# Scores and values in groups of four units: a fused top-k attention and leaky-ReLU MLP kernel on one core

## The chip, the cores and the metric

The kernel runs on one core of a Trainium2 chip. A core has five engines that run side by side, each with its own queue of instructions: PE (TensorE, matmuls; the loading of its stationary operand is listed as PEld), DVE (VectorE), ACT (ScalarE), POOL (GpSimd) and SP (SyncE, which issues the transfers here). They wait for each other by semaphores. The metric is the device time of one execution in microseconds (us); lower is better. The median of three runs before the change is 1473.3 us (1473.19 to 1473.83).

## What is computed

Top-k attention over 8 batches of 8 heads, 576 queries and keys of 64 elements, and then an MLP on its output, all in float32:

```python
scores = q @ k.T / sqrt(64)                      # (8, 8, 576, 576)
kth = the 32nd largest score of each row
scores = where(scores >= kth, scores, -1e9)
attn = softmax(scores)                           # with + 1e-9 in the denominator
x = (attn @ v), heads side by side               # (4608 tokens, 512)
h = x @ w_in                                     # (4608, 2048)
out = maximum(0.01 * h, h) @ w_out               # (4608, 512)
```

## The kernel before

The attention is cut into 144 *units*: 128 query rows of a pair of heads each (or, where 576 is no multiple of 128, 64 rows of two pairs: the *left* units, two at the end of each even batch and two at the start of each odd one). The tokens of the MLP are cut into *chunks*: two of 128 tokens, then seventeen of 256; eight units fill a chunk of 256. The host code only lays the inputs out.

What is done for a unit, cut to its instructions:

```python
def scores(us):                       # two units at a time
    narrow = ps_sc.tile([P, 2, 512], F32, name="narrow")            # PSUM
    for k, u in enumerate(us):
        wide = ps_sc.tile([P, 2, 512], F32, name="wide", bufs=2)    # PSUM, two buffers
    ...  # PE: q by k; u0 wide part, u0 narrow part, u1 narrow part, u1 wide part
    ...  # ACT: copies the four parts to u.both ("s_sb"), in the same order (L227)

def top_k(u):                         # DVE; yields after each of 4 rounds ("slots")
    pairs = max and min of the row's two halves                     # L250
    for r in range(4):
        nc.vector.max(u.tops[..r..], ...)                           # L255, both heads
        if r < 3: nc.vector.match_replace(...)                      # L258, both heads
        yield

def mask(u, i):                       # POOL, head i of the unit: needs the last top
    pen = (u.s[i] < kth) * MASKED; u.s[i] += pen                    # L268, L269

def exponents(u, i):                  # ACT
    u.s[i] = exp(SCALE * u.s[i] + nbias), row sum to u.z            # L272
def sums(u):        u.ze = u.z + 1e-9                               # ACT, L277
def reciprocals(u): u.rz = 1 / u.ze                                 # DVE, L281
def normalize(u, i): u.s[i] *= u.rz                                 # ACT, L284

def transpose(u):                     # by way of DRAM
    for h in range(2):                # the two 16-bit halves of each word
        nc.scalar.copy(split, pairs[:, :, h])                       # ACT, L293
        nc.sync.dma_start(apart[:, h, :], split)
    u.wT = work.tile([P, 2 * NKC - 1, P], F32, name="wT", bufs=3)
    nc.sync.dma_start_transpose(out=u.wT.bitcast(U16), in_=apart...)
# transpose_in_haste / keep_transposed: the same on PE and ACT, for units 15, 23, 31

def weigh_values(u, po): ...          # PE: v by wT into PSUM (L333); po is in a "wide" buffer
def keep_values(u, po): ...           # ACT: po to x, the MLP's input (L347)
```

The MLP is a generator that yields after every few matmuls, so that the main loop can spread it between the attention's parts:

```python
def hidden_of_few(x):                 # the two chunks of 128 tokens
    for j in range(NFC // 4 + 1):
        if j < NFC // 4:
            ...                       # PE: quarter j of x @ w_in into ph
            nc.scalar.activation(g_of[j], ph, AF.Prelu, alpha=SLOPE)
            yield 2 * 512
        if j:
            ...                       # PE: quarter j-1 turned into pt; ACT: copied to gT
            yield 2 * P

def mlp(ch):
    ...                               # chunks of 256: ph (L384), Prelu to gT (L390), 8 times
    for r0 in range(0, n, P):
        for f in range(NFC):
            ...                       # PE: pz += gT[f] by w_out[f] (L396)
        ...                           # ACT: o_sb <- pz (L403); transfer to out
```

And the main loop, one unit per step; the instructions of each engine run in this order:

```python
def values_at(n):
    if n < UNHURRIED:
        return (n | 1) + LAG + 1, MIDDLE
    return (n | 1) + LAG - ((n | 1) in HURRIED), END       # LAG = 3

for s in range(len(steps) + LAG + 1):
    cur, old, older, new = unit(s), unit(s - 1), unit(s - 2), ()
    if s % 2 == 0:
        new = [u for u in steps[s + 2:s + 4] if u]
    slot()                            # DVE: first round of top_k(cur)
    mask(old, 0); mask(old, 1)        # POOL
    weights_of(older)                 # DVE: reciprocals; ACT: normalize x2 (from step 20 on)
    mlp_steps(budget)
    ...                               # values(s, MIDDLE) of the early steps
    slot()
    mlp_steps(budget)
    exponents(old, 0)
    transpose(older)
    slot()
    mlp_steps(budget); mlp_steps(budget)
    slot()
    mlp_steps(budget)
    exponents(old, 1); sums(old)
    keep(values(s, END), s, END)      # PE: two units' values; ACT: copies to x
    if new: scores(new)               # PE and ACT
    mlp_steps(budget); mlp_steps(budget)
    load_more(s)
```

`budget` is the MLP work at hand by the slots (seven per step) that are left until the next chunk is complete.

Before all this the weights arrive as 64-bit words, through three raw buffers, and are rounded to float32.

Of the kernel before, what the change touches and what calls it, by code (L numbers as in the profile page):

```python
# [16 lines left out]
NKC = 5  # L17
# [3 lines left out]
def kernel(  # L21
# [39 lines left out]
    loads = ctx.enter_context(tc.tile_pool(name="loads", bufs=LOADED))  # L61
    raws = ctx.enter_context(tc.tile_pool(name="raws", bufs=3))
    work = ctx.enter_context(tc.tile_pool(name="work", bufs=2))
# [18 lines left out]
    gT = const.tile([P, NFC, CHMAX], F32, name="gT")  # L82

# [4 lines left out]
    def piece(n):  # L90
# [5 lines left out]
        return w_out[f // 4][:, f % 4:f % 4 + 2, :].rearrange("p g n -> p (g n)")  # L96

    raw_of = {}

    def load_weights(n):  # L100
        if n >= NPIECE:
            return
        if not AS_WORDS:
            nc.sync.dma_start(piece(n), weights[n])
            return
        raw_of[n] = raws.tile([P, WCH, 4], U16, name="raw")
        nc.sync.dma_start(raw_of[n].rearrange("p n w -> p (n w)"), weights[n])

    def round_weights(n):
# [8 lines left out]
        low = raw.rearrange("p n w -> p (n w)").bitcast(U32).rearrange("p (n w) -> p n w", w=2)[:, :, 0]  # L118
        top = raws.tile([P, WCH], U16, name="top", bufs=2)
        scale = raws.tile([P, WCH], U16, name="scale", bufs=2)  # L120
        parts = work.tile([P, 2 * NKC - 1, P], F32, name="wT", bufs=3)
        parts = parts.rearrange("p c n -> p (c n)").bitcast(U16)
        m_top, m_low = parts[:, 0:WCH], parts[:, WCH:2 * WCH].bitcast(BF16)
        nc.gpsimd.tensor_copy(top, raw[:, :, 3])
        nc.scalar.activation(dst, mid, AF.Copy, bias=-7.0 - 2.0 ** -16, scale=2.0 ** -20)

        nc.scalar.activation(m_low, low, AF.Copy, bias=128.0, scale=2.0 ** -29)
        yield
        nc.vector.tensor_scalar(scale, top, 4, 0x7FF, ALU.logical_shift_right, ALU.bitwise_and)
# [31 lines left out]
    def load_qk(pi):  # L161
        if pi % (LOADED + 3) < LOADED:
            qt = loads.tile([P, S], F32, name="qt")
            kt = loads.tile([P, S], F32, name="kt")
        else:
            raw = raws.tile([P, WCH, 4], U16, name="raw").rearrange("p n w -> p (n w)").bitcast(F32)
            qt, kt = raw[:, 0:S], raw[:, S:2 * S]
        nc.sync.dma_start(qt, qT[pi])
        nc.sync.dma_start(kt, kT[pi])
        qk_of[pi] = qt, kt  # L170
# [32 lines left out]
    def scores(us):  # L203


        narrow = ps_sc.tile([P, 2, 512], F32, name="narrow")
        ps = {}
        for k, u in enumerate(us):
            wide = ps_sc.tile([P, 2, 512], F32, name="wide", bufs=2)
            ps[u] = ((wide[:, :, 0:WIDE], 0, WIDE),  # L210
                     (narrow[:, :, k * NARROW:(k + 1) * NARROW], WIDE, S))

        order = ((us[0], 0), (us[0], 1), (us[1], 1), (us[1], 0))
        for u, part in order:
            to, k0, k1 = ps[u][part]
            for n in range(0, len(u.parts), 2):
                for i, pi, side, r0 in u.parts[n:n + 2]:
                    qt, kt = qk_of[pi]
                    d = slice(side * D, (side + 1) * D)
                    nc.tensor.matmul(to[r0:r0 + u.rows, i, :], qt[d, u.q0:u.q0 + u.rows],  # L220
                                     kt[d, k0:k1], start=True, stop=True)
        for u in us:
            u.both = work.tile([P, 2, S], F32, name="s_sb", bufs=5)
            u.s = [u.both[:, i, :] for i in range(2)]
        for u, part in order:
            to, k0, k1 = ps[u][part]
            nc.scalar.copy(u.both[:, :, k0:k1], to)  # L227

    def first_scores(u):

        ps = [ps_sc.tile([P, 2, 512], F32, name="wide", bufs=2) for i in range(2)]
        for half in range(2):
            for i, pi, side, r0 in u.parts:
# [3 lines left out]
                                 kt[d, half * HS:(half + 1) * HS], start=True, stop=True)  # L237
        u.both = work.tile([P, 2, S], F32, name="s_sb", bufs=5)
        u.s = [u.both[:, i, :] for i in range(2)]
        for i in range(2):  # L240
# [45 lines left out]
    def transpose(u):  # L286
# [4 lines left out]
        for h in range(2):  # L291
            split = work.tile([P, 2 * S], U16, name="split", bufs=2)
            nc.scalar.copy(split, pairs[:, :, h])  # L293
            nc.sync.dma_start(apart[:, h, :], split)
        u.wT = work.tile([P, 2 * NKC - 1, P], F32, name="wT", bufs=3)
        nc.sync.dma_start_transpose(out=u.wT.bitcast(U16), in_=apart.rearrange("p h n -> (p h) n"))
# [12 lines left out]
    def keep_transposed(u):  # L309
        u.wT = work.tile([P, 2 * NKC - 1, P], F32, name="wT", bufs=3)  # L310
        for c0, c1, pt in u.parts_T:
            nc.scalar.copy(u.wT[:, c0:c1, :], pt[:, 0:c1 - c0, :])
# [37 lines left out]

    def hidden_of_few(x):

        g_of = {}
        for j in range(NFC // 4 + 1):
            if j < NFC // 4:
                ph = ps_ml.tile([P, 512], F32, name="ph", tag="ml")
                for c in range(HP):
                    nc.tensor.matmul(ph, x[c][:, 0:P], w_in[c][:, j * 512:(j + 1) * 512],
                                     start=(c == 0), stop=(c == HP - 1))
                    if c == 1:  # L360
                        yield 2 * 512
                g_of[j] = raws.tile([P, 2 * DMODEL], U16, name="scale", bufs=2).bitcast(F32)
                nc.scalar.activation(g_of[j], ph, AF.Prelu, alpha=SLOPE)
                yield 2 * 512
            if j:
                pt = ps_ml.tile([P, 4, P], F32, name="pt", tag="ml")
                for i in range(4):
                    nc.tensor.transpose(pt[:, i, :], g_of[j - 1][:, i * P:(i + 1) * P], ident)
                nc.scalar.copy(gT[:, 4 * (j - 1):4 * j, 0:P], pt)
                yield 2 * P  # L370

    def mlp(ch):
# [4 lines left out]
        if ch < EARLY:  # L377
            yield from hidden_of_few(x)
        for f0 in range(0, NFC if ch >= EARLY else 0, 2):
# [12 lines left out]
        for r0 in range(0, n, P):  # L392
            m = min(P, n - r0)
            pz = ps_ml.tile([P, 512], F32, name="pz", tag="ml")
            for f in range(NFC):
# [4 lines left out]
                if f % 2 and f + 1 < NFC:  # L400
                    yield 2 * DMODEL
            o_sb = work.tile([P, DMODEL], F32, name="o_sb", bufs=1)
            nc.scalar.copy(o_sb[0:m], pz[0:m, 0:DMODEL])  # L403
# [30 lines left out]
    HURRY = 20  # L434
    HURRIED = (15, 23, 31)
    UNHURRIED = 14
    MIDDLE, END = 0, 1

    def values_at(n):

        if n < UNHURRIED:
            return (n | 1) + LAG + 1, MIDDLE
        return (n | 1) + LAG - ((n | 1) in HURRIED), END

# [18 lines left out]

    def slot_budget(s):

        after = [at for (at, _), _ in ready_at if at >= s]
        until = after[0] if after else s
        if len(after) >= len(CHUNKS) - EARLY:
            return EARLY_SHARE
        return backlog[0] / ((until + 1 - s) * SLOTS)  # L470

    EARLY_SHARE = 500
    SLOTS = 7

    with tc.manual_schedule():
        last = {p: n for n, u in enumerate(steps) for p in u.pairs}

        def load_more(s):

            for of, load, n, lag in ((v_of, load_v, LOADED_V, LAG + 1), (qk_of, load_qk, LOADED + 3, 8)):  # L480
                while len(of) < NPAIR and (len(of) < n or last[len(of) - n] + lag <= s):
                    load(len(of))
                    if lag > LAG + 1 and len(of) > n:
                        break

# [4 lines left out]
        for n in range(NPIECE + 2):  # L490
            for i in (n, n - 1, n - 2) if AS_WORDS else ():
                if 0 <= i < NPIECE:
                    if i == n:
                        rounding[i] = round_weights(i)
                    next(rounding[i], None)
# [16 lines left out]
        def values(*place):  # L512
            due = [u for n, u in enumerate(steps) if values_at(n) == place]
            if due:
                po = ps_sc.tile([P, 2, 512], F32, name="wide", bufs=2)[:, 0, 0:2 * P]
                po = po.rearrange("p (u n) -> p u n", u=2)
            else:
                return ()
# [9 lines left out]
        for s in range(len(steps) + LAG + 1):  # L528
            cur, old, older, new = unit(s), unit(s - 1), unit(s - 2), ()
            if s % 2 == 0:  # L530
                new = [u for u in steps[s + 2:s + 4] if u]
            picks = top_k(cur) if cur else iter(())
            budget = slot_budget(s)

            def slot():
                next(picks, None)

            slot()
            if old:
                mask(old, 0)  # L540
                mask(old, 1)
            late = s < HURRY and not {s - 1, s - 2} & set(HURRIED)
            if older and not late:
                weights_of(older)
# [6 lines left out]
            if older and late:  # L551
                weights_of(older)
            if s - 2 in HURRIED:
                transpose_in_haste(older)
            mlp_steps(budget)
            if old:
                exponents(old, 0)
            if older:
                keep_transposed(older) if s - 2 in HURRIED else transpose(older)
            slot()  # L560
# [77 lines left out]
```

## Time and profile before

| | |
|---|---|
| median time | 1473.3 us |
| span of the profiled run | 1471.7 us |
| busy: PE, DVE, ACT, POOL | 1395.9, 1322.2, 1096.5, 1096.0 us |
| mean granted PE clock | 0.979 |
| PE busy in the first 240 us | 170.2 us |
| PE busy from 240 to 1400 us | 1157.9 of 1160 us |
| first to last top-k instruction on DVE | 64.7 to about 1385 us |

The busy share is a mean over stages. The table parts it: in the first 240 us the weights are loaded and rounded, and the first chunks wait for their units; after that PE has hardly a gap. The profile's queries used below are: the timeline (instructions of one engine in order of time, start and length in us, equal ones merged, with the idle time before them and what ended it), the waits (who waited for whom: us in total, times, longest) and the windows (busy time of each engine in a stretch, with the granted PE clock).

### The profile page before, as it was taken

The numbers are of one execution on the slowest core, as the hardware profiler recorded it, in microseconds if no ns is written. First come the engines' busy times: TensorE is split into PE (matmuls) and PEld (weight loads), VectorE is DVE, ScalarE is ACT, GpSimd is POOL, SyncE is SP. The second block draws the span as 40 slices with busy tenths as digits, with TensorE's granted clock in tenths as the row PEclk, the third lists the DMA queues.
The fourth block names the chain that finished last, engine by engine and source line by source line (L and its number), as shares of the span: only waits on it lengthen the run. The fifth ranks groups of instructions, "written<-read, shape, count | busy, mean of one in ns | idle before, by whom it ended". The sixth has DMA issues, their size and how long they took to land.

```text
span 1471.7 us, 24082 instructions
## 1 busy us (share of the span) xinstructions
PE 1395.9 (95%) x8059; PEld 928.4 (63%) x8059; DVE 1322.2 (90%) x3400; ACT 1096.5 (75%) x1979; POOL 1096.0 (74%) x743
## 2 busy tenths in 40 slices
PE   7717989999999999999999999999999999999998
PEld 2304547676767666666666666666666767676674
DVE  6999998999999999999999999999999999999600
ACT  8557877877787777777777777777777787877710
POOL 3288887888788888787878787888887888787600
PEclk9957999999999999999999999999999999999999
DMA  9725453654367554665466545565467655654510
GB/s 350 280 78 132 138 143 89 172 169 139 103 172 209 138 141 130 184 183 144 134 174 187 155 128 147 163 194 143 128 168 205 145 136 131 167 137 131 144 47 14
DMA packets 391419, 223.47 MB, mean 152 GB/s; under 512 B 336256, under 2 KB 336256, under 8 KB 389248
## 3 DMA queue, kind: packets, MB, share of 16 engines
q1 hardware_dynamic: 391296, 221.95, 54.0%
q8 instruction: 63, 1.03, 0.3%
q14 instruction: 60, 0.49, 0.1%
HBM read 46.14 MB, written 92.60 MB: 94 GB/s over the span
## 4 chain that ended last, share of the span: by engine, by line
PE 84%; DVE 10%; DMA 3%; ACT 2%; issue 1%; SPq 0%; POOL 0%; DVEq 0%; ACTq 0%
PE ph L384 32%; PE pz L396 32%; PE wide L333 11%; PE wide L220 6%; DVE tops L255 4%; PE narrow L220 3%; DVE pairs L258 3%; DMA wT<-apart 1%; DVE pairs L250 1%; DMA raw<-in_weights_dram 1%; DVE w_in L155 1%; ACT split L293 1%; DVE scale L152 1%; ACT s_sb L284 0%; DMA apart<-split 0%
## 5 line engine op out<-in xcount | busy, mean ns | idle before, releaser
L268 POOL TENSOR_SCALAR pen<-s_sb,tops 128x576 f32<-128x576 f32 x288 | 637.5, 2213 | 210.9 <-DVE tops L255 123.6
L255 DVE MAX8 tops<-pairs 128x8 f32<-128x288 f32 (+1 forms) x1152 | 636.3, 592 | 0.0
L396 PE MATMUL pz<-w_out,gT 128*128 128x512 f32 x1152 | 508.9, 596 | 0.0
L384 PE MATMUL ph<-x,w_in 128*128 128x256 f32 x2176 | 481.1, 381 | 0.0
L258 DVE MATCH_REPLACE8 pairs<-tops,pairs 128x288 f32<-128x288 f32 (+1 forms) x864 | 460.5, 538 | 0.0
L384 PEld LDWEIGHTS ph<-x,w_in 128*128 128x128 f32 x2176 | 410.7, 190 | 77.1 <-issue 22.9
L269 POOL TENSOR_TENSOR s_sb<-s_sb,pen 128x576 f32<-128x576 f32 x288 | 406.3, 1411 | 24.1
L396 PEld LDWEIGHTS pz<-w_out,gT 128*128 128x128 f32 x1152 | 215.6, 190 | 266.6 <-issue 264.6
L293 ACT COPY split<-s_sb 128x1152 uint16<-128x1152 uint16 x282 | 309.1, 1144 | 0.0
L284 ACT ACTIVATE s_sb<-s_sb,rz 128x576 f32<-128x576 f32 x288 | 207.0, 769 | 40.3 <-DVE rz L281 40.1
L272 ACT ACTIVATE s_sb<-s_sb,nbias 128x576 f32<-128x576 f32 x288 | 220.9, 767 | 12.5 <-POOL s_sb L269 12.5
L250 DVE TENSOR_TENSOR pairs<-s_sb 128x576 f32<-128x576 f32 x288 | 213.2, 779 | 9.9
L333 PEld LDWEIGHTS wide<-wT,vt 128*64 128x64 f32 x3200 | 161.8, 139 | 67.7 <-ACT s_sb L227 26.3
L333 PE MATMUL wide<-wT,vt 128*64 128x128 f32 (+1 forms) x3200 | 179.6, 269 | 24.4 <-ACT s_sb L227 21.2
L390 ACT ACTIVATE gT<-ph 128x512 f32<-128x512 f32 x136 | 80.5, 592 | 80.1 <-PE ph L384 80.1
L347 ACT COPY x<-wide 128x128 f32<-128x128 f32 (+1 forms) x160 | 32.1, 260 | 131.9 <-PE wide L333 131.9
L227 ACT COPY s_sb<-wide 128x704 f32<-128x704 f32 x142 | 107.1, 754 | 23.8 <-PE wide L220 23.8
L220 PE MATMUL wide<-kt,qt 64*128 64x352 f32 (+1 forms) x392 | 77.0, 509 | 26.5 <-ACT s_sb L227 23.6
L227 ACT COPY s_sb<-narrow 128x448 f32<-128x448 f32 x142 | 68.7, 536 | 1.4 <-PE narrow L220 0.7
L403 ACT COPY o_sb<-pz 128x512 f32<-128x512 f32 x36 | 21.0, 584 | 59.3 <-PE pz L396 59.3
L281 DVE RECIPROCAL rz<-ze 128x2 f32<-128x2 f32 x144 | 22.4, 156 | 47.0 <-ACT ze L277 46.8
L258 DVE MATCH_VALUE_LOAD pairs<-tops,pairs 128x8 f32 x864 | 63.1, 73 | 0.0
(63 smaller groups left out, 620.1 us busy)
## 6 DMA issues: line engine op xcount, KB each, us to landing
apart<-split SPq DMA_DIRECT2D x282, 288.0 KB, 2.1
raw<-in_weights_dram SPq DMA_DIRECT2D x16, 1024.0 KB, 6.4
vt<-in_vk_dram SPq DMA_DIRECT2D x32, 320.0 KB, 3.4
out_dram<-o_sb SPq DMA_DIRECT2D x36, 256.0 KB, 2.0
qt<-in_qT_dram SPq DMA_DIRECT2D x20, 288.0 KB, 3.3
kt<-in_kT_dram SPq DMA_DIRECT2D x20, 288.0 KB, 3.6
raw<-in_qT_dram SPq DMA_DIRECT2D x12, 288.0 KB, 3.3
raw<-in_kT_dram SPq DMA_DIRECT2D x12, 288.0 KB, 3.7
```

The costliest lines, as they stand in the source:

```text
L220: nc.tensor.matmul(to[r0:r0 + u.rows, i, :], qt[d, u.q0:u.q0 + u.rows], kt[d, k0:k1], start=True, stop=True)
L250: nc.vector.tensor_tensor(pairs[:, :, n, :], u.both[:, :, 0:HS], u.both[:, :, HS:S], op)
L255: nc.vector.max(out=u.tops[:, i, r, :], in_=rest[i])
L258: nc.vector.match_replace(out=rest[i], in_to_replace=u.tops[:, i, r, :], in_values=rest[i], imm_value=LOWEST)
L268: nc.gpsimd.tensor_scalar(pen, u.s[i], u.tops[:, i, ROUNDS - 1, 7:8], MASKED, ALU.is_lt, ALU.mult)
L269: nc.gpsimd.tensor_tensor(u.s[i], u.s[i], pen, ALU.add)
L272: nc.scalar.activation(u.s[i], u.s[i], AF.Exp, bias=u.nbias[:, i:i + 1], scale=SCALE, accum_out=u.z[:, i:i + 1])
L284: nc.scalar.activation(u.s[i], u.s[i], AF.Copy, bias=0.0, scale=u.rz[:, i:i + 1])
L293: nc.scalar.copy(split, pairs[:, :, h])
L333: nc.tensor.matmul(po[side * D:(side + 1) * D, o, :], vt[:, c, side, :], u.wT[:, c + side * NKC if c + 1 < NKC else c, r:r + n], start=(c ...
L384: nc.tensor.matmul(ph[:, i, 0:n], w_in[c][:, f * P:(f + 1) * P], x[c][:, 0:n], start=(c == 0), stop=(c == HP - 1),)
L396: nc.tensor.matmul(pz[0:m, 0:DMODEL], gT[:, f, r0:r0 + m], w_out[f // 4][:, f % 4, :], start=(f == 0), stop=(f == NFC - 1),)
```

## The change

From unit 36 on the values of four units are weighed together, and from unit 40 on the scores of four units are computed around them, in every fourth step and earlier in the step: scores of two units, values of four, scores of two. The purpose is fewer changes between the three kinds of matmul on PE. Values that wait longer need more buffers: five of the transposed weights and six of the scores. They are laid into the raw weights' memory, which is free once the weights are rounded, so the raw buffers become named tiles. Besides, in the two small chunks the last quarter of the hidden layer is turned after the eighth matmul of the second layer instead of before its first; unit 14 is turned on PE too; and in step 17 the reciprocals of unit 15 come first.

The core of the diff (cut: the renaming of buffers, loads, `late` in `hidden_of_few`):

```diff
+    later = words.rearrange("p a n -> p (a n)").bitcast(F32)
+    wT_bufs = [work.tile(..., name=f"wT{n}", bufs=1) for n in range(3)]
+    wT_bufs += [t.rearrange("p (c n) -> p c n", n=P) for t in later[3:5]]
+    s_bufs = [work.tile([P, 2, S], F32, name=f"s_sb{n}", bufs=1) for n in range(5)]
+    s_bufs += [last_scores.rearrange("p (i n) -> p i n", i=2)]
...
     def mlp(ch):
...
                 if f % 2 and f + 1 < NFC:
                     yield 2 * DMODEL
+                if f == 7 and ch in few:
+                    yield from turned(NFC // 4 - 1, few[ch])
...
+    HASTY = (14, 15, 23, 31)
-    MIDDLE, END = 0, 1
+    MIDDLE, END, AMID = 0, 1, 2
+    FOURS = 40
     def values_at(n):
+        if n >= FOURS - 4:
+            return ((n | 1) if len(steps[n].pairs) > 1 and n % 4 < 2 else (n | 3)) + LAG + 1, AMID
...
-            if s % 2 == 0:
-                new = [u for u in steps[s + 2:s + 4] if u]
+            if s % 2 == 0 and s + 2 < FOURS:
+                new = steps[s + 2:s + 4]
+            four = s % 4 == 3 and s + 1 >= FOURS
...
+            at_first = s < HURRY and s - 2 in HURRIED
+            if at_first:
+                weights_of(older)
             slot()
...
             mlp_steps(budget)
             if old:
                 exponents(old, 0)
+            if not four:
+                keep(values(s, AMID), s, AMID)
+            else:
+                if unit(s + 1):
+                    scores(steps[s + 1:s + 3])
+                keep(values(s, AMID), s, AMID)
+                budget = slot_budget(s, SLOTS_AHEAD)
             if older:
-                keep_transposed(older) if s - 2 in HURRIED else transpose(older)
+                keep_transposed(older) if s - 2 in HASTY else transpose(older)
+            if four and unit(s + 3):
+                scores(steps[s + 3:s + 5])
             slot()
             mlp_steps(budget)
             mlp_steps(budget)
```

The value product still takes one of the two "wide" buffers of PSUM, in turn with the scores.

## The prediction

> **What bounds the kernel now.** First the page's busy line and, from the windows, the dense stretch:
>
> ```profile
> PE 1395.9 (95%) x8059; PEld 928.4 (63%) x8059; DVE 1322.2 (90%) x3400; ACT 1096.5 (75%) x1979; POOL 1096.0 (74%) x743
> ...
> 240.00:1400.00 1160.00, 1157.87 (x6943) 793.29 (x6942) 1099.60 (x2862) 913.56 (x1685) 935.12 (x626) 1.00 0.57 155
> ```
>
> From 240 to 1400 us PE (second busy figure) lacks 2.1 us. DVE fills 95%, so it is only some 5% behind. Next, PE's timeline over one period of two units:
>
> ```profile
> 710.85 2.40 PE L333 MATMUL wide<-wT,vt 128*64 128x128 f32 x40
> 713.18 0.86 PE L220 MATMUL wide<-kt,qt 64*128 64x352 f32 x4
> 713.88 0.92 PE L220 MATMUL narrow<-kt,qt 64*128 64x224 f32 x8
> 714.64 0.76 PE L220 MATMUL wide<-kt,qt 64*128 64x352 f32 x4
> 715.33 1.99 PE L384 MATMUL ph<-x,w_in 128*128 128x256 f32 x8
> 717.16 12.18 PE L396 MATMUL pz<-w_out,gT 128*128 128x512 f32 x28
> 729.27 2.40 PE L333 MATMUL wide<-wT,vt 128*64 128x128 f32 x40
> ```
>
> Values 2.33 us, scores 2.15, MLP 13.94, without a gap: 18.42 us for two units, 36.84 for four. PE is the bound. But what does DVE wait for? In the waits, DVE's largest is:
>
> ```profile
> DVE rz L281 <- ACT ze L277: 46.8, 52, 6.9
> ```
>
> And in the timelines of DVE and then ACT, one step:
>
> ```profile
> 719.96 1.45 DVE L250 TENSOR_TENSOR pairs<-s_sb 128x576 f32<-128x576 f32 x2
> ...
> 723.17 0.17 DVE L281 RECIPROCAL rz<-ze 128x2 f32<-128x2 f32 x1 [0.18 <-ACT ze L277]
> ...
> 729.03 1.52 DVE L250 TENSOR_TENSOR pairs<-s_sb 128x576 f32<-128x576 f32 x2
> ```
>
> ```profile
> 719.94 2.19 ACT L293 COPY split<-s_sb 128x1152 uint16<-128x1152 uint16 x2
> 722.03 0.78 ACT L272 ACTIVATE s_sb<-s_sb,nbias 128x576 f32<-128x576 f32 x1
> ...
> 722.94 0.20 ACT L277 ACTIVATE ze<-z 128x2 f32<-128x2 f32 x1
> 723.37 1.44 ACT L284 ACTIVATE s_sb<-s_sb,rz 128x576 f32<-128x576 f32 x2 [0.23 <-DVE rz L281]
> ```
>
> The reciprocal stands in DVE's queue after the first round of the next unit's top-k. DVE's step takes 8.9 us (719.96 to 729.03 less the wait of 0.18), and rz falls due 3.03 us into it (722.99). ACT gave ze 0.2 us after that: there is no slack between ACT's ze and DVE's next step.
>
> [...] DVE sits idle 0.18 us before rz, though the next max waits for nothing of ACT's. [...] the change sets three groups in a row on two "wide" buffers. [...] the third figure from the end is the clock:
>
> ```profile
> 194.00:198.00 4.00, 0.00 (x0) 0.00 (x0) 3.97 (x8) 4.00 (x7) 2.79 (x4) 0.94 0.40 111
> 198.00:202.00 4.00, 3.80 (x32) 2.27 (x36) 4.00 (x14) 2.80 (x7) 3.82 (x3) 0.50 0.36 119
> 202.00:206.00 4.00, 4.00 (x17) 1.50 (x10) 4.00 (x10) 3.54 (x6) 2.80 (x4) 0.70 0.58 128
> ```
>
> **Part 1, what it removes.** Each change of the kind of matmul costs PE about 0.2 us: 28 pz matmuls in a row take 12.02 us, so 32 should take 13.74, but 32 after scores take 13.93 (all in the chain of waits). Before, four units have six changes (MLP to values to scores to MLP, twice); after, four. That is 0.4 us less for four units, PE's loop falls to 36.45 us, and over 25 groups 10 us would be saved if PE stayed the bound.
>
> **Part 2, what it moves.** In the order of the built program, ACT has in every fourth step: normalize x2, exponents (head 0), four score copies, four x copies, two splits, four score copies, exponents (head 1), ze. Before, all score and x copies stood behind ze. Now ze stands behind them, and rz of the next DVE step waits for it. With D the start of that DVE step, and every duration from the timelines of 700 to 745 us:
>
> - rz(previous unit) at D+3.03; normalize starts 0.20 later (723.17 to 723.37), D+3.23.
> - Normalize takes 1.33 (717.85 to 719.18), exponents 0.76: the first copies start at D+5.32. POOL's mask of head 0 is done earlier, about D+3.15 (719.96 to 723.11).
> - First wide copy 0.75, all four 2.38 (714.09 to 716.47): D+6.07 and D+7.70.
> - The values take the wide buffer that this first copy empties. PE, which by then has slack, waits and starts at about D+6.2. Forty matmuls 2.33; the next forty without a change 2.16: D+10.7.
> - The x copies start 0.12 after the last value matmul (713.18 to 713.30) and take 0.215 each: D+11.7. PE is already at the second scores, until D+12.9.
> - Splits 2.09, D+13.8; four score copies 2.38, D+16.1; exponents 0.91, D+17.05; ze and the hop to rz 0.23: rz at D+17.3.
>
> Due was D+8.9+3.03 = D+11.93. DVE stands still 5.35 us in one of four steps; every second group has a Prelu (0.49) between normalize and exponents, so 5.6 on average. DVE's loop is 4 x 8.9 + 5.6 = 41.2 us, against 36.84 now: +4.4 us. There are 25 such groups (steps 43 to 139; step 39 has no values yet and comes to 1.2 us of wait, which DVE's 1.2 us of slack in four steps takes). 25 x 4.4 = +109 us.
>
> **Part 3, what follows on PE.** PE has 36.45 us of work in 41.2, and its gap of about 4.7 us lies in one piece, before the values. It is as long as the gap shown, whose cost was 4 x 0.5 + 4 x 0.3 = 3.2 us of PE time. The values lie in that very chain, so each such half clock adds up to 3.2 us to DVE's wait. I take it for half of the groups, by judgement: 12.5 x 3.2 = +40 us.
>
> **Part 4, start and end.** The late quarter removes PE's 4.24 us gap at 194 us and the slow clock behind it; but DVE's step 17 starts at 215.27, and the values of units 14 and 15 at 227.2 can't come before its rz, normalize and the turning, about 223.5. So at most 3.7; I take 3. At the end DVE stops 85 to 88 us before the last instruction now (1384.9 of 1471.7); after, the last values come in step 147, with 28 MLP slots of 1 us, 4.5 of values and a chunk of 55 behind step 143: about the same, I take 3 less. Longer lags of the values cost nothing: wT is ready at about 18 us after the start of the unit's second step (split end 710.5, transfers some 8), and the values come later than before.
>
> **Sum.** 1473.3 + 109 + 40 - 6 = 1616. As my chain takes every wait at its longest (copies may start per unit, not per group), I set 1600.
>
> **Rivals.** (a) What was meant: PE stays the bound, 1473 - 10 - 6 = 1457. For it speaks that PE is 95% busy and ACT only 75%; against it that the order on ACT puts 11 us of its own work between one rz and the next, whatever PE does. (b) ACT's own work alone is in the chain, PE's values never are: 0.2 + 1.33 + 0.76 + 2.38 + 0.86 + 2.09 + 2.38 + 0.91 + 0.23 = 11.1, so rz at D+14.2, 2.3 us of wait, 2.5 with the Prelu: the loop is 38.1, +1.3 x 25 = +31, about 1498. It fails if the values need the buffer that the first copy empties, as the order of the buffers says. (c) The half clock strikes in every group: +109 + 80 - 6, about 1656. (d) Transposes or loads late for the larger groups: waits on DMA of 5.2 us in all now, and later need dates; I give it nothing.
>
> **Range and chances.** From (b), with some of the values' wait, to (c): 1540 to 1655. Faster needs the ACT order to cost nothing: 0.03. Within 2%, that is below 1503, is (b) or less: 0.10. Slower: 0.87.
>
> **What would show it.** Right: "DVE rz <- ACT ze" grows from 46.8 to 170 us or more, in waits of 4 us and over, one in four steps; PE has gaps of 3 to 5 us before its values that end on ACT's copies; the period of four units is 40 to 45 us; the granted clock falls below 0.97. Wrong: PE without gaps and a period of 36.4 us (a), rz waits of about 2 us (b), or long waits on wT (d). A period near 41 at full clock would leave Part 2 right and Part 3 wrong.

## The result and the profile after

The changed kernel takes 1610.5 us in the median (1609.3 to 1611.5) against 1473.2 before: a ratio of 1.0934, with a 95% interval from 1.0916 to 1.0953. In its code the lines have moved: scores are L243 and their copies L249, values L354 and their copies L368, exponents L293, ze L298, the reciprocal rz L302, normalize L305, splits L314, the MLP's ph L410 and pz L422.

The page's busy line and, from the windows, the stretch in which the groups of four run (columns as before: length, then the busy time of PE, PEld, DVE, ACT and POOL, the PE clock, the DMA share, GB/s):

```profile
PE 1435.9 (89%) x8066; PEld 976.6 (61%) x8068; DVE 1322.6 (82%) x3400; ACT 1084.8 (67%) x1979; POOL 1096.0 (68%) x743
...
420.00:1500.00 1080.00, 984.53 (x5607) 690.34 (x5607) 906.91 (x2363) 734.22 (x1367) 767.22 (x513) 0.95 0.49 136
```

DVE, ACT and POOL do the same work as before, to within 1% or so. PE lacks 95 us in this stretch, although its own busy time has grown by 40: part of it ran at a slower clock (the granted clock is 0.95 in this stretch, the third figure from the end, and 0.947 on the mean of the run, where it was 0.979). The kernel is no longer bound by any one engine. The waits say by what (who waited for whom: us in total, times, longest):

```profile
DVE rz L302 <- ACT ze L298: 183.6, 35, 8.3
...
PE wide L354 <- ACT s_sb L249: 115.7, 27, 13.6
```

The first was 46.8 us before. One group of four, in the timelines of PE, then DVE, then ACT:

```profile
837.43 0.92 PE L243 MATMUL narrow<-kt,qt 64*128 64x224 f32 x8
838.19 0.76 PE L243 MATMUL wide<-kt,qt 64*128 64x352 f32 x4
843.11 2.40 PE L354 MATMUL wide<-wT,vt 128*64 128x128 f32 x20 [4.16 <-ACT s_sb L249]
845.29 3.84 PE L354 MATMUL wide<-words,vt 128*64 128x128 f32 x40
848.97 1.26 PE L354 MATMUL wide<-wT,vt 128*64 128x128 f32 x20
850.16 0.86 PE L243 MATMUL wide<-kt,qt 64*128 64x352 f32 x4
...
886.02 3.98 PE L354 MATMUL wide<-wT,vt 128*64 128x128 f32 x40 [3.85 <-ACT s_sb L249]
```

```profile
836.55 1.51 DVE L271 TENSOR_TENSOR pairs<-s_sb 128x576 f32<-128x576 f32 x2
839.56 0.15 DVE L302 RECIPROCAL rz<-ze 128x2 f32<-128x2 f32 x1
845.48 1.43 DVE L271 TENSOR_TENSOR pairs<-s_sb 128x576 f32<-128x576 f32 x2
856.35 0.17 DVE L302 RECIPROCAL rz<-ze 128x2 f32<-128x2 f32 x1 [7.86 <-ACT ze L298]
```

```profile
841.57 0.76 ACT L293 ACTIVATE s_sb<-s_sb,nbias 128x576 f32<-128x576 f32 x1
842.24 0.19 ACT L293 ACTIVATION_READ_ACCUMULATOR s_sb<-s_sb,nbias 128x1 f32 x1
842.33 0.73 ACT L249 COPY s_sb<-wide 128x704 f32<-128x704 f32 x1
...
850.28 0.77 ACT L368 COPY x<-wide 128x128 f32<-128x128 f32 x4 [5.71 <-PE wide L354]
850.91 2.24 ACT L314 COPY split<-tops_scales 128x1152 uint16<-128x1152 uint16 x2
853.02 0.78 ACT L249 COPY s_sb<-wide 128x704 f32<-128x704 f32 x1
...
855.14 0.84 ACT L293 ACTIVATE s_sb<-s_sb,nbias 128x576 f32<-128x576 f32 x1
...
856.11 0.20 ACT L298 ACTIVATE ze<-z 128x2 f32<-128x2 f32 x1
```

Read across the three: D is 836.55. PE has its first scores done by 839 and waits 4.16 us for ACT's first score copy, which ACT can start only at 842.33, after normalize and exponents. Then ACT waits 5.71 us for the values, and ze comes at 856.11. DVE stands before rz for 7.86 us. From these values to the next (843.11 to 886.02) four units take 42.9 us, in place of 36.84.

The clock in the same group (windows; third figure from the end):

```profile
836.00:840.00 4.00, 2.94 (x20) 1.82 (x18) 3.97 (x12) 1.36 (x5) 3.77 (x3) 1.00 0.85 286
840.00:844.00 4.00, 0.89 (x8) 0.89 (x10) 4.00 (x13) 4.00 (x9) 3.70 (x3) 0.69 0.63 138
844.00:848.00 4.00, 4.00 (x42) 4.00 (x40) 3.90 (x10) 0.57 (x1) 3.03 (x2) 0.50 0.55 161
848.00:852.00 4.00, 4.00 (x54) 3.43 (x50) 0.49 (x3) 1.72 (x6) 3.82 (x3) 0.96 0.00 0
```

The values ran slowly: from 843.11 to 850.16 the granted clock was 0.63 on the mean (0.50 from 844 to 848 us), and they took 7.05 us. The same work took 4.51 us in the group whose values start at 928.47, at a granted clock of 1.00.

The loss can be summed from DVE's timeline: 25 groups, each followed by a wait for ze, 2.6 to 8.3 us long, together 166 us. DVE had 4 x 8.9 = 35.6 us of work in PE's old period of 36.84, so 25 x 1.24 = 31 us of slack. 166 - 31 = 135 us, beside a measured 137.

### The profile page after: what moved, and what is told of

The parts are those of the page before. It is cut to its first block, busy times and chain, and to the rows that moved or that the text cites. A ratio compares the mean times of both kernels' runs of the same rounds, so it can differ in the third digit from the quotient of the medians.

```text
span 1608.4 us, 24108 instructions
## 1 busy us (share of the span) xinstructions
PE 1435.9 (89%) x8066; PEld 976.6 (61%) x8068; DVE 1322.6 (82%) x3400; ACT 1084.8 (67%) x1979; POOL 1096.0 (68%) x743
## 4 chain that ended last, share of the span: by engine, by line
DVE 48%; PE 32%; ACT 15%; issue 4%; DMA 1%; POOL 0%; DVEq 0%; SPq 0%; ACTq 0%
DVE tops L276 23%; DVE pairs L279 17%; PE wide L354 12%; PE pz L422 11%; PE ph L410 6%; DVE pairs L271 5%; ACT s_sb L249 4%; ACT split L314 3%; ACT s_sb L293 3%; ACT s_sb L305 2%; PE wide L243 1%; DMA words<-in_weights_dram 1%; ACT x L368 1%; ACT tops_scales L305 1%; DVE rz L302 1%
## 5 line engine op out<-in xcount | busy, mean ns | idle before, releaser
L289 POOL TENSOR_SCALAR pen<-s_sb,tops 128x576 f32<-128x576 f32 x250 | 553.3, 2213 | 322.0 <-DVE tops L276 165.3
L422 PE MATMUL pz<-w_out,gT 128*128 128x512 f32 x1152 | 504.2, 595 | 4.2 <-ACT tops_scales L383 4.2
L410 PE MATMUL ph<-x,w_in 128*128 128x256 f32 x2176 | 477.0, 380 | 1.6 <-ACT gT L416 1.2
L410 PEld LDWEIGHTS ph<-x,w_in 128*128 128x128 f32 x2176 | 411.2, 190 | 69.0 <-issue 9.6
L422 PEld LDWEIGHTS pz<-w_out,gT 128*128 128x128 f32 x1152 | 216.1, 190 | 273.4 <-issue 268.2
L290 POOL TENSOR_TENSOR s_sb<-s_sb,pen 128x576 f32<-128x576 f32 x250 | 352.8, 1411 | 20.9
L305 ACT ACTIVATE s_sb<-s_sb,rz 128x576 f32<-128x576 f32 x250 | 180.0, 769 | 170.5 <-DVE rz L302 170.5
L314 ACT COPY split<-s_sb 128x1152 uint16<-128x1152 uint16 x242 | 266.1, 1151 | 0.0
L354 PE MATMUL wide<-wT,vt 128*64 128x128 f32 (+1 forms) x1920 | 137.8, 312 | 83.4 <-ACT s_sb L249 83.3
L293 ACT ACTIVATE s_sb<-s_sb,nbias 128x576 f32<-128x576 f32 x250 | 194.1, 777 | 11.2 <-POOL s_sb L290 11.2
L271 DVE TENSOR_TENSOR pairs<-s_sb 128x576 f32<-128x576 f32 x250 | 186.3, 784 | 7.8 <-DVE tops L276 0.5
L354 PEld LDWEIGHTS wide<-wT,vt 128*64 128x64 f32 x1920 | 128.0, 167 | 102.3 <-ACT s_sb L249 95.4
L302 DVE RECIPROCAL rz<-ze 128x2 f32<-128x2 f32 x144 | 22.3, 155 | 183.7 <-ACT ze L298 183.6
L368 ACT COPY x<-wide 128x128 f32<-128x128 f32 (+1 forms) x160 | 29.9, 266 | 152.5 <-PE wide L354 152.5
L354 PE MATMUL wide<-words,vt 128*64 128x128 f32 (+1 forms) x1280 | 89.3, 304 | 34.8 <-ACT s_sb L249 32.4
L354 PEld LDWEIGHTS wide<-words,vt 128*64 128x64 f32 x1280 | 81.9, 163 | 45.1 <-ACT s_sb L249 39.1
L289 POOL TENSOR_SCALAR pen<-tops_scales,tops 128x576 f32<-128x576 f32 x38 | 84.1, 2213 | 24.5 <-DVE tops L276 21.6
L243 PE MATMUL wide<-kt,qt 64*128 64x352 f32 (+1 forms) x392 | 75.4, 498 | 27.7 <-ACT s_sb L249 24.0
L249 ACT COPY s_sb<-wide 128x704 f32<-128x704 f32 x123 | 93.6, 761 | 7.6 <-PE wide L243 7.6
```

Of the source, the lines that this page charges most:

```text
L271: nc.vector.tensor_tensor(pairs[:, :, n, :], u.both[:, :, 0:HS], u.both[:, :, HS:S], op)
L289: nc.gpsimd.tensor_scalar(pen, u.s[i], u.tops[:, i, ROUNDS - 1, 7:8], MASKED, ALU.is_lt, ALU.mult)
L290: nc.gpsimd.tensor_tensor(u.s[i], u.s[i], pen, ALU.add)
L293: nc.scalar.activation(u.s[i], u.s[i], AF.Exp, bias=u.nbias[:, i:i + 1], scale=SCALE, accum_out=u.z[:, i:i + 1])
L305: nc.scalar.activation(u.s[i], u.s[i], AF.Copy, bias=0.0, scale=u.rz[:, i:i + 1])
L354: nc.tensor.matmul(po[side * D:(side + 1) * D, o, :], vt[:, c, side, :], u.wT[:, c + side * NKC if c + 1 < NKC else c, r:r + n], start=(c ...
```

## The experiments

The theory, "order": ze stands on ACT behind all the copies of the group (eight of scores, four of x, two splits), and rz on DVE waits for it. The rivals: "buffer" (PE's wait for the wide buffer is the bound, whatever ze does), "places" (the new memory places are slow), "clock" as a part of its own.

### ze first

```diff
                 if unit(s + 1):
                     scores(steps[s + 1:s + 3])
+                if old:
+                    exponents(old, 1)
+                    sums(old)
                 keep(values(s, AMID), s, AMID)
...
-            if old:
+            if old and not four:
                 exponents(old, 1)
                 sums(old)
```

> The changed kernel, but in every fourth step the exponents of head 1 and ze stand on ACT before the x copies (after the first four score copies), not behind all ten copies. Theory 'order' (DVE's rz waits for a ze that stands behind the copies on ACT): ze comes at about D+8.8 us of the DVE step, before rz is due at D+11.9, so the waits of 6 to 8 us vanish, PE is the bound again with about 36.5 us for four units: 1455 to 1470 us. Rival 'buffer' (the values' wait for the wide buffer is the bound in itself, ze or not): PE keeps gaps of about 4 us before the values, and the time stays at 1580 or more. Rival 'places' (the new places of the buffers or the larger groups are slow as such): 1550 or more.

Measured 1530.0 us (ratio to before 1.0389, 1.0369 to 1.0409): 80 of the 137 us are back, and none of the theories gave this number. "Places" and "buffer" can't be the whole, but "order" isn't either. In this run's waits, rz still waits 104.8 us, and another line has grown, from 57.5 us in the changed kernel:

```profile
ACT o_sb L431 <- PE pz L422: 138.5, 34, 13.2
```

The timelines of DVE and ACT behind one of its groups (D of the fourth step is 1041.52):

```profile
1053.40 0.15 DVE L302 RECIPROCAL rz<-ze 128x2 f32<-128x2 f32 x1
1059.24 1.52 DVE L271 TENSOR_TENSOR pairs<-s_sb 128x576 f32<-128x576 f32 x2
1065.71 0.17 DVE L302 RECIPROCAL rz<-ze 128x2 f32<-128x2 f32 x1 [3.38 <-ACT ze L298]
...
1076.00 0.17 DVE L302 RECIPROCAL rz<-ze 128x2 f32<-128x2 f32 x1 [1.33 <-ACT ze L298]
```

```profile
1065.91 1.44 ACT L305 ACTIVATE s_sb<-s_sb,rz 128x576 f32<-128x576 f32 x2 [0.23 <-DVE rz L302]
1071.52 0.59 ACT L431 COPY o_sb<-pz 128x512 f32<-128x512 f32 x1 [4.17 <-PE pz L422]
```

The rz right behind the group (1053.40) no longer waits. The ones one and two steps later do. ACT still has to finish the copies (it works without a gap from the x copies at 1055.46 to the end of ze at 1065.67, hence the 3.38 us), and then it stands for 4.17 us before an output copy of the MLP: PE's step with the group holds 8.8 us of attention besides its seven MLP slots, so PE is behind, and ACT waits for PE in a copy that stands ahead of the next exponents and ze in its queue. (These exponents start at 1072.00, though POOL's last instruction for their input, at 1066.34, took 0.23 us.) This suggests a second coupling: the *burst* on PE. PE's gap has not gone either: 3.54 us before the values of this group.

### Splits first

```diff
-                keep(values(s, AMID), s, AMID)
+                summed = values(s, AMID)
+                if older:
+                    transpose(older)
+                keep(summed, s, AMID)
...
-            if older:
+            if older and not four:
                 keep_transposed(older) if s - 2 in HASTY else transpose(older)
```

> The changed kernel, but in every fourth step the two splits stand on ACT before the x copies, so that ACT does them while it waits for the values; ze stays last. Theory 'order': 2.1 us leave the chain between one rz and the next, the wait falls by 2.1 us per group plus what less slow clock gives: 25 groups x 2.1 = 53, so 1520 to 1558 us. Rival 'buffer': the values start as late as before, the period of four units stays, 1600 or more.

Measured 1558.7 us (1.0587, 1.0568 to 1.0606), 51.8 us less than the changed kernel: 2.07 us for each of 25 groups, where two splits take 2.09. That the two agree so well is partly luck. At full clock the wait before rz falls by 1.87 us (5.33 to 3.46, 4.84 to 2.97); besides, the granted clock from 500 to 1300 us is 0.97 in place of 0.95, and new waits of 0.5 to 1.9 us appear one or two steps later. "Buffer" as the whole is out: the values start as late as before (6.1 or 6.6 us after D), and yet the time falls.

### Both

The two diffs together.

> Both: ze and the splits stand before the x copies. Theory 'order': no long rz wait, no gap on PE, and nothing late in the step after; 1452 to 1465 us, below the kernel before by the saved switches (25 groups x 0.4 us = 10) and the earlier start (3). Rival 'buffer': above 1580. If switches cost less than I think, 1465 to 1472.

Measured 1536.7 us (1.0433, 1.0418 to 1.0447), 6.7 us more than with ze first alone, and not the 1460 that "order" alone would give. With ze ahead of the splits, these aren't in the chain any more. The burst is the candidate for what is left (the waits "ACT o_sb <- PE pz" are 157.5 us); PE also still has gaps of 1.3 or 2.9 to 3.5 us before the values of full groups (6.6 at the first).

### No groups of four

`FOURS = 1000`: everything else of the change stays.

> The changed kernel with groups of two throughout (the groups of four never begin): left are the last quarter turned amid the second layer, unit 14 turned on PE, unit 15's reciprocal first, and the buffers' new places. Theory 'order': all loss is in the groups of four, so this runs at 1468 to 1473 us, some 3 below the kernel before. Rival 'places': above 1500.

Measured 1475.2 us (1.0018, 1.0009 to 1.0027). All of the loss but 2.4 us is in the groups. The start brings nothing. The timeline of PE says why:

```profile
194.31 0.60 PE L394 MATMUL pt<-ident,tops_scales 128*128 128x128 f32 x4
199.16 3.78 PE L422 MATMUL pz<-w_out,gT 128*128 128x512 f32 x4 [4.24 <-ACT tops_scales L383]
```

The 4.24 us gap of before is still there. The late quarter is out of the way, but the second layer's pz takes one of two PSUM buffers that ph, pt and pz share, and the releaser is the Prelu that empties ph. So the gap now stands before pz. That it is the buffer follows from the order of the allocations and the releaser; no run gave pz another buffer.

### More work on PE, in the gap

```diff
+                if unit(s + 1) and s >= FOURS:
+                    warm = ps_ml.tile([P, 512], F32, name="warm", tag="ml")
+                    for n in range(7):
+                        nc.tensor.matmul(warm[:, 0:256], w_in[0][:, 0:P], w_in[1][:, 0:256],
+                                         start=True, stop=True)
                 keep(values(s, AMID), s, AMID)
```

> The changed kernel with added work: in every group of four, seven more matmuls of 256 columns (14 records of 0.216 us, 3.0 us; nobody reads their result) stand on PE between the first two units' scores and the values, in the gap in which PE waits for ACT. Theory 'clock' (the gap of about 4 us brings the half clock, and the values behind it take 6.1 to 7.0 us in place of 4.5): the gap shrinks to about 1 us, the values take 4.5 us again, and with 42 us more of work on PE the kernel gets faster by 25 x 1.6 to 2.5: 1550 to 1575 us, mean clock back at 0.97 or more. Rival (the values are slow for another reason, their buffers or the transfers): 1605 to 1650 us.

Measured 1571.4 us (1.0675, 1.0661 to 1.0690): with 3 us more of useless matmuls in each group (75 us in all; the 42 of the expectation is a wrong product), the kernel is 39 us faster than the changed one. PE's timeline in this run:

```profile
1029.70 3.29 PE L611 MATMUL warm<-w_in,w_in 128*128 128x256 f32 x14
1033.40 1.31 PE L354 MATMUL wide<-wT,vt 128*64 128x128 f32 x20 [0.41 <-ACT s_sb L249]
1034.54 2.35 PE L354 MATMUL wide<-words,vt 128*64 128x128 f32 x40
1036.72 1.26 PE L354 MATMUL wide<-wT,vt 128*64 128x128 f32 x20
1037.91 0.86 PE L243 MATMUL wide<-words 64*128 64x352 f32 x4
```

The values take 4.51 us (1033.40 to 1037.91), the granted clock from 500 to 1300 us is 1.00 in place of 0.95, and the waits before rz behind full groups are 4.5 to 5.3 us. The first group alone still has a gap of 4.36 us and a wait of 6.5. So the run parts the 137 us as 39 for the clock, 2 for the rest of the change, and 96 for the chain at full clock. The 39 is what is left after the added matmuls' own cost: in the three groups that weigh the values of two left units the clock was whole anyway (1.00 in the changed kernel), and there they only raise the waits, from 2.6 to 3.1 us to 4.4 to 4.7. An estimate group by group from DVE's waits, against the same groups in this run (with 4.84 us for the first), gives 47 us for the clock (21 slow groups, 2.2 us each) and 89 for the chain.

### Even steps on PE

No MLP slots behind the group in its step; the slots before it and the other three steps take that work (`slots_by` counts two slots in a step with a group, seven in others).

```diff
-                budget = slot_budget(s, SLOTS_AHEAD)
+                budget = 0.0
...
-            budget = slot_budget(s + 1)
-            mlp_steps(budget)
-            mlp_steps(budget)
+            if not four:
+                budget = slot_budget(s + 1)
+                mlp_steps(budget)
+                mlp_steps(budget)
```

> The changed kernel without MLP slots after the attention group of every fourth step; the other three steps take a third more each, so that PE's steps are about equally long (about 10.8 and 8.5 us in place of 15.5 and 7). ACT's order in the group is as in the changed kernel. Theory 'order and burst' (the ze behind the copies, and besides it MLP evictions on ACT that wait for a PE which a burst of attention work has put behind): the rz wait behind the copies stays, so 1570 to 1615 us. Rival 'burst alone' (only PE's uneven steps matter): 1480 or less.

Measured 1594.2 us (1.0833, 1.0819 to 1.0848): with ACT's order as changed, even steps bring 16 us. The burst alone explains little; it matters once ze is out of the chain. Both together:

> ze and the splits before the x copies, and no MLP slots after the group in that step. Theory 'order and burst': with both couplings gone DVE's waits for ze are below 1 us each, PE has no gap before the values and is the bound at 36.5 us for four units: 1458 to 1475 us. If PE's wait for the first score copy is a third bound of its own: 1500 or more, with gaps of 3 us and over before the values.

Measured 1494.9 us (this is run e7; 1.0157, 1.0143 to 1.0170), 42 us below the same ACT order with the burst, but 20 above the top of what I expected. The waits before rz were 107.3 us with the burst; now they are less than in the kernel before:

```profile
DVE rz L302 <- ACT ze L298: 38.1, 31, 8.2
```

The run shows that the uneven steps cost these 42 us, not by which path. "ACT o_sb <- PE pz" has hardly shrunk (157.5 to 147.4 us), so its total is no measure of the burst. And PE now comes later to the group: its gaps before full groups' values are 0 or 1.3 us (but for the first, 9.1), and the granted clock from 500 to 1300 us is 1.00. PE's busy time falls by 15 us (1404.8 to 1389.3), so fewer gaps and less slow clock can be a good part of the 42 us. With the start as before the change:

> As the one before (ze and splits early, even slots), with the start as it was before the change: the last quarter turned before the second layer, unit 14 by way of DRAM, unit 15's reciprocal after the first round. The run without groups of four was 2.4 us above the kernel before, so the start's changes should be worth -2 here: 2 us below e7, 1456 to 1473. If the new places of the buffers cost those 2.4 us, it equals e7.

Measured 1494.8 us (run e8; 1.0155, 1.0141 to 1.0169): the start's changes are worth nothing either way. Its PE timeline has one gap of 9.1 us where the groups of four begin, and then one of 1.3 us in about eight units, in turn with a DVE wait of about 1.2 us for a late score copy: PE came to its groups now too early, now too late, since the last two slots of a step were budgeted as if two slots fewer were left.

```diff
-                budget = slot_budget(s + 1)
+                budget = slot_budget(s, SLOTS - 2) if s + 1 >= FOURS else slot_budget(s + 1)
```

> As e8 (ze and splits early, no MLP slots after the group, start as before the change), with the last two slots of a step budgeted by the slots that really are left, so that PE has 26.8 and 28.3 us of MLP between groups in turn, not 25.8 to 29.4. e8's trace has a gap of 9.1 us on PE at 452 us, where the first values of four come (the chunk of units 32 to 39 is complete half a step later than in pairs, and PE has run out of MLP), and then about 1.3 us of gap in eight units. If the gaps in eight units come from the uneven pacing: 1480 to 1488 us. If from the order itself: 1493 to 1496. Either way not below the kernel before.

Measured 1478.7 us (1.0038, 1.0025 to 1.0050). PE's windows and timeline in this run:

```profile
420.00:480.00 60.00, 50.48 (x265) 32.09 (x262) 59.09 (x158) 45.29 (x83) 50.84 (x35) 0.91 0.66 181
500.00:1300.00 800.00, 797.45 (x4855) 550.27 (x4852) 769.59 (x2002) 632.87 (x1167) 650.45 (x436) 1.00 0.57 157
```

```profile
827.50 0.86 PE L243 MATMUL wide<-kt,qt 64*128 64x352 f32 x4
...
829.64 2.40 PE L354 MATMUL wide<-wT,vt 128*64 128x128 f32 x40
831.88 2.35 PE L354 MATMUL wide<-words,vt 128*64 128x128 f32 x40
...
836.30 27.03 PE L405 MATMUL ph<-x,w_in 128*128 128x256 f32 x124
```

From 500 to 1300 us PE is the bound again, and here is what the change was for: scores, values and scores take 8.80 us (827.50 to 836.30); before, two pairs took 2 x 4.48 = 8.96 and one more return to the MLP (0.19). 0.35 us are saved for four units, and eight units take 73.0 us from values to values (829.64 to 902.65) in place of 73.7. Over 25 groups that would be about 8 us, an estimate. The values still share the two wide buffers with the scores, and behind the first group PE has no gap before them: the buffer was no bound in itself. But the gap at the transition costs 9.5 us and some slow clock (PE is busy 50.5 of 60 us, at a granted clock of 0.91), and the rest of the change 2. No run beat the kernel before.

### Groups of four from unit 92

`FOURS = 92`: 12 groups in place of 25, two of them with the values of left units (of the 25, three).

> The changed kernel with groups of four from unit 92 instead of 40: 12 full groups in place of 25. The loss should go with their number: 1475 (no groups) + 12/25 of 135 us = 1540, 1530 to 1550. If a good part of the loss is paid once, at the change from two to four, it is 1555 or more.

Measured 1538.3 us (1.0442, 1.0425 to 1.0459): the loss over 1475.2 is 63.1 us, 5.3 for each group, where 25 groups lose 5.4 each. It is paid by the group, not once.

### The 2.4 us outside the groups

Groups of two throughout; first with only the late quarter left of the start's changes (`HASTY = HURRIED`, `at_first = False`), then with the start wholly as before.

> Groups of two throughout, and of the change at the start only the last quarter turned amid the second layer (unit 14 by way of DRAM, unit 15's reciprocal after the first round, as before). The run without groups of four was 2.4 us above the kernel before. If turning unit 14 on PE costs that, this is 1471 to 1473; if the late quarter or the buffers' places cost it, 1474 to 1476.

> Groups of two throughout and the start wholly as before the change: left are the buffers' new places alone (named tiles in the raw weights' memory, five wT and six score buffers, the later POOL copy in the order). Expected to equal the kernel before, 1471.5 to 1473; 1474 or more if the places cost the 2.4 us.

Measured 1475.4 us (1.0015, 1.0006 to 1.0023) and 1474.7 (1.0016, 1.0010 to 1.0022): neither unit 14 nor the quarter costs it. It is in the buffers' places or what came with them. The second run's profile has a value product that waits longer for its transposed weights than any before (0.80 us there):

```profile
601.60 1.61 PE L354 MATMUL wide<-wT,vt 128*64 128x64 f32 x40 [2.30 <-DMA wT<-apart]
```

The first of the three kernels (no groups of four) waits at most 0.9 us for them, and takes the same time. So what costs the 2 us stays open.

## Why the prediction held, step by step

**Part 1** (PE's switches): 0.4 us for four units predicted, 0.35 measured, in the run where PE is the bound. It doesn't show in the changed kernel, as foreseen.

**Part 2** (the chain on ACT) is right in its mechanism, and nearly in its size. For the group above, with D = 836.55 and a Prelu in it: the first copy starts at D+5.78 (predicted 5.32 + 0.49), the values at D+6.56 (6.2 + 0.49). At full clock most waits are 4.84 us, or 5.33 with a Prelu, predicted 5.35 and 5.85. Two terms were mis-sized: the second four score copies hold ACT 2.12 us and not 2.38, and the four x copies 0.63 us and not 0.86. Most of this is a slip in reading: I counted to the end of the last copy, but ACT's next instruction starts before that (850.91 against 850.28 + 0.77, 855.14 against 855.32), and for x I doubled such a length. And a count was wrong: three groups weigh the values of two left units only (the other pair goes alone, two steps earlier), and their waits are 2.6 to 3.1 us. Chain at full clock: +89 us by the estimate above (+96 by the run with added matmuls), where I said +109.

**Part 3** (half clock): +39 us by the run, +47 by the estimate, where I said +40, but by two errors that cancel. I gave it half of the groups at 3.2 us each. The timeline shows slow values behind 21 of 25 gaps (at a granted clock of 0.59 to 0.75), so about 1.9 or 2.2 us each.

**Part 4** failed at the start: the gap at 194 us did not go, it moved from before the last turn to before pz, and what lies outside the groups costs 2 us. I said -6 for start and end together.

**The sum** was 1616 and I set 1600, for copies that may start per unit. The x copies started per group: all four stand together behind the last value matmul, 5.71 us after ACT was free. The correction was not needed. That 1616 came so near to 1610.5 is luck: by the estimate the chain was 20 us too long, the clock 7 too small and the start and end 8 too hopeful, and these nearly cancel.

**The rivals**: (a) is out in the changed kernel. (b), ACT's own work alone, is out: ACT waited for PE's values before the x copies of every group, 3.2 to 6.1 us in full ones, 1.1 in those with left units. (c) was nearer in number of groups than in cost. (d) is out: PE's longest wait for transposed weights is 1.3 us.

**Missed in the reasoning**: I treated ze's place as the only thing that holds DVE, so I expected ze first to heal all. The burst of attention work on PE costs as well: in the timelines of ze first it holds ACT's MLP copies (4.17 us before the one at 1071.52), and these hold the next ze. In the changed kernel the first coupling hides the second.

## What to carry to other kernels

When a group of instructions is moved in an engine's queue, look at the small result that now stands behind it, and who waits for it a step later (here DVE for ze, 2.6 to 8.3 us in each group): the engine's busy share (75% here) says nothing of that. Move the small result ahead of the bulk copies, do independent work while the engine would wait for another (the splits under the values: 52 us here while ze stood last, no gain once ze stood ahead), and then even out the work that the other engines' results wait behind. A group that gathers work also delays what it completes: here the first chunk came half a step later, and that single gap of 9.5 us ate what the fewer switches saved.

## What the runs showed of the hardware

The length of a PE gap alone did not tell in the changed kernel whether the matmuls behind it ran slowly. Of its 25 groups, 22 had a gap of 3.48 to 7.58 us before the values. Behind 21 of these gaps the values took 5.94 to 7.46 us, at a granted clock of 0.59 to 0.75 over that time. Behind one of 3.53 us the same work took 4.51 us at a granted clock of 1.00, and the rz wait of that group is the shortest of the full groups, 5.33 us. Behind the two shortest, 3.48 us each, the values took 5.95 us at 0.75 and 7.38 at 0.60. Behind the three gaps of 1.3 to 1.5 us, before the values of left units, the granted clock was 1.00. Why the gap of 3.53 us differs from the others was not shown. Filling most of the gap with matmuls that nobody needs made the kernel 39 us faster.
